# The output's columns taken with a stride of four, stores of whole 512-byte runs, and a written order for three engines in the last layers of an fp32 attention and two-MLP kernel

## The chip, the core and the metric

One NeuronCore of a Trainium2 chip runs the whole program. The metric is device time of one execution in microseconds (us). A change of less than about 0.3% (3.5 us here) can't be told from none.

## What is computed

```python
def _attn_ref(q, k, v, mem_k, mem_v):          # (4, 8, 768, 64), 8 memory slots
    for c in range(768 // 32):                 # chunks of 32 queries, window 16 + 32 + 8
        ...
        a = softmax(scale * q_c @ concat(mem_k, k_ctx).T)
        out[:, :, c_start:c_end] = a @ concat(mem_v, v_ctx)

x = attn_out.transpose(0, 2, 1, 3).reshape(3072, 512)
h = x @ w_in                                   # 512 x 2048
x = np.maximum(0.01 * h, h) @ w_out            # 2048 x 512
y = ((x @ w_a) * (x @ w_b)) @ moe2_w_out       # 512 x 1536, twice, then 1536 x 512
```

All arrays are fp32; y has 3072 rows (tokens) of 512 columns, so a row is 2 KB.

## The kernel before

**Numbers.** An fp32 operand is kept as two parts, `hi` (a rounded copy) and `lo` (the rest), and a product is three matmuls: lo·hi, hi·lo, hi·hi. ScalarE (ACT) makes `hi` with a cast, VectorE (DVE) makes `lo` with a subtraction.

**Stages.** Attention and the first MLP run over six blocks of 512 tokens (`TB`). Beside them `prep_steps` (L676) reads w_a, w_b and the second w_out, forms the sums of their quarters that a seven-product scheme (Strassen's, in Winograd's form) needs, splits them and stores them in DRAM (`wabd`, `wtd`). The scheme replaces the eight products of a 2 by 2 block product by seven, numbered `i` = 0 to 6.

**The last layers.** They run over three super-blocks `sb` of 1024 tokens (two halves `h` of 512), and in each over six pairs `p` of 128-column tiles of w_a and w_b. For a pair, `layer3(k, m)` (L885) makes the seven products with w_a (`m` = 0), then the seven with w_b (`m` = 1), six matmuls of 512 columns each. They go to the PSUM banks `ca`, `cb`, `cc`; a bank goes on being summed into after ACT has copied its state into a tile `u` (`snap`, L892): `u2` after product 4, `u3` after product 5. So PE may start product 5 only after the `u2` copy, and product 2 only after the `u3` copy. DVE combines banks and copies into `ga` (w_a side) and, multiplied by it, `gb`. The four `gb` quarters then give seven operands `st`: ACT casts (`cast`, L900), DVE subtracts (`low`, L906), with four DVE additions between them (c22, c21, c11, c12).

Two pairs form a group `g`. Its output product is 14 units (`unit`, L1033): 7 products for each of two 128-column tiles `dt` of w_out, six matmuls each into `oa`, `oy` or `oz`, after which DVE (or ACT, for the first group) adds the bank to `acc`. Units of a group run between the products of the next pair; a super-block's last group runs among the first products of the next super-block, or alone at the end of the program.

**The change of super-block.** The operands of the next super-block (`xc_make`, L755: `ch` by ACT, `cl` by DVE, `t1` to `t4` by DVE, each of 1024 columns) are made while the last group runs. Finished `acc` tiles are transposed by DVE in 32 by 32 blocks (`turn`, L1043) into `y` and stored: for each of the eight (h, e, dt) tiles of a super-block four stores of 32 columns by 512 tokens, 64 KB each, in runs of 32 columns, 128 bytes. This happens during the next super-block's pairs 0 and 1, or at the end of the program.

**What sets the order.** PE follows the order of the text in all of this part (`InOrder`, L31, `pe.on`). DVE and ACT follow it only around the ends of super-blocks (`dve.on`, `act.on`); elsewhere the framework's scheduler orders them by priority. SyncE (SP) issues all loads and stores, in the order that the scheduler gave: weights `wab` (512 KB, two products each, a ring of 5 tiles, `wab_load` L838), output weights `wt` (`wt_load` L859), the `xs` loads and the stores. A DMA whose buffer or data is not ready holds up every later one on SP. Which products and units alternate is written in the table `PLAN` (L1066) and the main loop (L1075).

Of the kernel before, what the change touches and what calls it, by code (L numbers as in the profile page):

```python
# [14 lines left out]
P = 128  # L15
# [38 lines left out]
def kernel(  # L54
# [621 lines left out]
    def prep_steps():  # L676
        n = 0
        for p in range(NF2 // 2):
            for m in range(3):
# [6 lines left out]
                z11, z12 = z[:, 0, 0:256], z[:, 0, 256:512]  # L686
                z21, z22 = z[:, 1, 0:256], z[:, 1, 256:512]
# [8 lines left out]

                def comb(c, x, y, op):
                    nc.vector.tensor_tensor(out=t[:, c], in0=x, in1=y, op=op)
# [8 lines left out]
                else:  # L707
                    plain(0, 1, z11)
                    plain(1, 2, z[:, 1, :])
# [38 lines left out]
    def xc_parts(sb, i, t):  # L748
        hi = xq.tile([P, HC, TB], F32R, tag=f"ch{i}", name=f"ch{i}")
        lo = xq.tile([P, HC, TB], F32R, tag=f"cl{i}", name=f"cl{i}")  # L750
        two = "p k n -> p (k n)"
        w_parts(hi.rearrange(two), lo.rearrange(two), t.rearrange(two), dve)
        xc[sb, i] = (hi, lo)

    def xc_make(sb, i):  # L755
# [7 lines left out]
        if i == "t1":  # L763
            sub(b12, b12, b11)
        elif i == "t2":
            sub(b12, b22, b12)
        elif i == "t3":
            sub(b11, b12, b11)
        elif i == "t4":
            sub(b21, b21, b12)  # L770
        else:
            xc_parts(sb, i, (b11, b21, b21, b12, b12, b11, b22)[i])
# [110 lines left out]
    ga, gb, later = {}, {}, {}  # L883

    def layer3(k, m):  # L885
# [4 lines left out]
        ends = p == NP - 1  # L890
# [19 lines left out]
        def done(k, h, ps, t=None):  # L910
# [24 lines left out]
            c11, c12, c21, c22 = gb[0, 0], gb[1, 0], gb[0, 1], gb[1, 1]  # L935
            if not ends or sb + 1 < NS:
                low(1, c12)
            tt(c22, c21, c22, ALU.add)
            cast(3, c22)
            tt(c21, c11, c21, ALU.subtract)  # L940
            low(3, c22)
            tt(c11, c22, c11, ALU.subtract)
            cast(4, c11)
            tt(c12, c12, c11, ALU.subtract)
            low(4, c11)
            cast(6, c12)
            cast(5, c21)
# [24 lines left out]
        u2 = snap(A, "u2")  # L972
        yield
# [7 lines left out]
        if m and ends:  # L981
            later[2] = lambda: low(2, gb[1, 1])
# [3 lines left out]
        if m and ends:  # L986
            later[1] = lambda: low(1, gb[1, 0])
        yield
        product(C, n + 6, sb, 6, False)
        done(0, 1, C, u2)  # L990
        yield
        if m:
            low(6, gb[1, 0])
            low(5, gb[0, 1])
# [4 lines left out]
    def mul(sb, g, dt, i, seed=False):  # L999
        if i == 0:  # L1000
# [11 lines left out]
        for k in range(2):  # L1012
            c, w = st[sb, 2 * g + k, i], wts[sb, g, i][:, k]
            kw = dict(skip_group_check=True)
            pe.matmul(ps, w[:, 1, q], c[:, 0], start=begins and k == 0, stop=False, **kw)
            pe.matmul(ps, w[:, 0, q], c[:, 1], start=False, stop=False, **kw)
            pe.matmul(ps, w[:, 0, q], c[:, 0], start=False, stop=k == 1, **kw)
# [3 lines left out]
    def add(sb, g, dt, i):  # L1021
# [4 lines left out]
        acc = accs[sb, h][:, e, dt]  # L1026
        ps = {3: oy, 6: oy, 1: oz}.get(i, oa)[dt]
# [33 lines left out]
    def stage(k, m, pos):  # L1061
        if made.get((k, m), 0) == pos:
# [3 lines left out]
    PLAN = (  # L1066
        {3: ((0, 0),), 4: ((0, 3), (0, 1)), 5: ((0, 4),)},
        {
            0: ((0, 6),), 6: ((0, 5),), 7: ((1, 0), (0, 2)), 2: ((1, 3), (1, 4)),
            3: ((1, 1), (1, 5)), 4: ((1, 6), (1, 2)),  # L1070
        },
    )

    pe.on, pe.last = True, None
    for k, (sb, p) in enumerate(pairs):  # L1075
# [3 lines left out]
        for m in range(2):  # L1079
            end = p == NP - 1 and m == 1  # L1080

            def units(pos):
                if not odd and p:
                    for u in PLAN[m].get(pos, ()):
                        unit(sb, g - 1, *u)

            for pos in range(6):
                held = p == 4 and sb + 1 < NS and m == 0 and pos == 5
                if held:
                    dve.on, dve.last = True, None  # L1090
                stage(k, m, pos)
                if held:
                    xc_make(sb + 1, "t1")
                    dve.on = False
                units(pos)
                if pos == 1 and (k or m):
                    for e in (6, 7, 8):
# [168 lines left out]
```

## Time and profile before

| | |
|---|---|
| median of 3 runs | 1169.02 us (1168.79 to 1171.77) |
| the profiled execution, its own time | 1166.6 us |
| its span, first to last instruction | 1164.8 us |
| PE busy | 1117.6 us, 96% |
| DVE, ACT busy | 722.1 us (62%), 498.2 us (43%) |
| last layers | from about 606 us to the end |
| stores of the output | 53.4 thousand packets of less than 512 bytes in the last layers, queue issues 96 x 64 KB |

The profile is one execution. Its page gives busy shares by engine, slices in time and a chain of waits followed back from the last instruction; the trace behind it gives windows, timelines of single instructions and DMA queues. Matmul ends are modelled (0.39 us shown for one that the next follows after 0.227 us), so idle times of PE in the rows are short of the time lost by 0.16 us; the start of one row and of the next is the safer measure.

### The profile page before, as it was taken

The page shows a single profiled execution, that of the slowest core. Times are in us where ns is not written, and L with a number is a line of the kernel's source. Part 1 is how long each engine was busy: PE and PEld are TensorE (multiplying, and loading weights), DVE is VectorE, ACT ScalarE, POOL GpSimd, SP SyncE. Part 2 cuts the span into 40 slices and gives each one's busy share as a digit, 9 for nine tenths or more (in the row PEclk, how much of TensorE's full clock was granted, in tenths as well). Part 3 has the DMA queues.
Part 4 walks back from the last instruction along what each step waited for, and adds up shares of the span by engine and source line. Part 5 has one row for each costly group of instructions (what it writes and reads, how often), then busy time and mean ns, then how long its engine had stood idle before and what let it go on. Part 6 is the DMA issues. An engine that isn't in the chain of part 4 may idle for free.

```text
span 1164.8 us, 16365 instructions
## 1 busy us (share of the span) xinstructions
PE 1117.6 (96%) x6236; PEld 918.6 (79%) x6236; DVE 722.1 (62%) x1325; ACT 498.2 (43%) x831; POOL 6.3 (1%) x16
## 2 busy tenths in 40 slices
PE   7899999999999999999999999999799999799994
PEld 6788888888878888888888888877688887588873
DVE  6896588779768946544105556678446578436574
ACT  5886555455455543343223432324333233334140
POOL 2000000000000000000000000000000000000000
PEclk9999999999999999999999999999899999899997
DMA  9996899999999984244339474767774766856534
GB/s 315 392 357 227 289 327 331 336 314 335 326 319 335 321 293 136 92 178 166 115 138 329 144 247 139 243 189 173 234 235 145 236 181 172 213 178 208 177 99 72
DMA packets 136462, 269.58 MB, mean 231 GB/s; under 512 B 59840, under 2 KB 60992, under 8 KB 135616
## 3 DMA queue, kind: packets, MB, share of 16 engines
q1 hardware_dynamic: 136304, 268.41, 70.3%
q8 instruction: 49, 0.80, 0.3%
q14 instruction: 29, 0.24, 0.1%
q10 hardware_dynamic: 80, 0.13, 0.0%
HBM read 214.50 MB, written 54.00 MB: 231 GB/s over the span
## 4 chain that ended last, share of the span: by engine, by line
PE 87%; DVE 4%; DMA 3%; ACT 3%; SPq 1%; issue 0%; DVEq 0%; ACTq 0%
PE ca L47 14%; PE oa L47 8%; PE h L410 8%; PE a L530 7%; PE a L534 7%; PE a L533 7%; PE h L411 7%; PE h L412 7%; PE cc L47 7%; PE oy L47 4%; PE cb L47 4%; DVE gb L898 3%; PE pv L383 2%; PE s L274 2%; DMA wab<-wab 2%; PE oz L47 1%
## 5 line engine op out<-in xcount | busy, mean ns | idle before, releaser
L47 PE MATMUL ca<-ch,wab 128*128 128x512 f32 x575 | 198.8, 398 | 18.1 <-DMA wab<-wab 14.7
L410 PE MATMUL h<-xh,w 128*128 128x512 f32 (+1 forms) x384 | 151.5, 395 | 0.7 <-ACT xh L47 0.7
L530 PE MATMUL a<-gh,w 128*128 128x512 f32 (+1 forms) x392 | 150.7, 384 | 0.8 <-ACT x L547 0.8
L533 PE MATMUL a<-gl,w 128*128 128x512 f32 (+1 forms) x392 | 150.4, 384 | 0.0
L534 PE MATMUL a<-gh,w 128*128 128x512 f32 (+1 forms) x392 | 150.4, 384 | 0.0
L411 PE MATMUL h<-xl,w 128*128 128x512 f32 (+1 forms) x384 | 148.5, 387 | 0.2 <-DVE xl L47 0.2
L412 PE MATMUL h<-xh,w 128*128 128x512 f32 (+1 forms) x384 | 148.5, 387 | 0.0
L47 PEld LDWEIGHTS ca<-ch,wab 128*128 128x128 f32 x575 | 109.6, 191 | 48.7 <-DMA wab<-wab 16.6
L508 DVE TENSOR_TENSOR gl<-g,gh 128x512 fp32r<-128x512 f32 (+1 forms) x96 | 65.4, 681 | 104.6 <-ACT gh L505 100.5
L47 PE MATMUL ca<-cl,wab 128*128 128x512 f32 x288 | 113.7, 395 | 1.5 <-DVE cl L47 1.5
L903 ACT CAST st<-gb 128x512 fp32r<-128x512 f32 x111 | 67.5, 621 | 107.3 <-DVE gb L898 104.9
L502 ACT ACTIVATE g<-h 128x512 f32<-128x512 f32 (+1 forms) x96 | 56.3, 587 | 128.2 <-PE h L412 127.2
L47 PE MATMUL oa<-st,wt 128*128 128x512 f32 x432 | 106.9, 389 | 0.0
L47 PE MATMUL cc<-ch,wab 128*128 128x512 f32 x288 | 100.4, 389 | 0.0
L47 PEld LDWEIGHTS oa<-st,wt 128*128 128x128 f32 x432 | 80.9, 188 | 17.2 <-DVE acc L47 0.4
L530 PEld LDWEIGHTS a<-gh,w 128*128 128x128 f32 x392 | 73.6, 188 | 16.1 <-ACT x L547 1.5
L534 PEld LDWEIGHTS a<-gh,w 128*128 128x128 f32 x392 | 73.7, 188 | 14.5
L533 PEld LDWEIGHTS a<-gl,w 128*128 128x128 f32 x392 | 73.6, 188 | 14.5
L410 PEld LDWEIGHTS h<-xh,w 128*128 128x128 f32 x384 | 72.1, 188 | 16.3 <-ACT xh L47 0.8
L898 DVE TENSOR_TENSOR st<-gb,st 128x512 fp32r<-128x512 f32 x108 | 73.2, 689 | 17.3 <-ACT st L903 16.5
L412 PEld LDWEIGHTS h<-xh,w 128*128 128x128 f32 x384 | 72.1, 188 | 14.7
L411 PEld LDWEIGHTS h<-xl,w 128*128 128x128 f32 x384 | 72.2, 188 | 14.2 <-DVE xl L47 0.5
(155 smaller groups left out, 1627.6 us busy)
## 6 DMA issues: line engine op xcount, KB each, us to landing
wab<-wab SPq DMA_DIRECT2D x126, 512.0 KB, 4.4
w<-wod SPq DMA_DIRECT2D x80, 512.0 KB, 4.6
raw<-w SPq DMA_DIRECT2D x68, 512.0 KB, 7.0
wt<-wtd SPq DMA_DIRECT2D x63, 512.0 KB, 4.4
k<-kl SPq DMA_DIRECT2D x48, 256.0 KB, 5.2
v<-vl SPq DMA_DIRECT2D x48, 256.0 KB, 5.1
wab<-pwb SPq DMA_DIRECT2D x12, 768.0 KB, 6.9
wod<-w SPq DMA_DIRECT2D x16, 512.0 KB, 6.4
```

Source lines behind the costliest of these rows:

```text
L47: self.last = emit(*args, **kwargs).ins
L274: pe.matmul(s[64 * cpar:64 * cpar + 64, cp * 4 + hp, :], qb[:, o, :], k[:, r:r + 64], start=True, stop=True,)
L410: pe.matmul(ps, w[1], x[0], start=first, stop=False)
L411: pe.matmul(ps, w[0], x[1], start=False, stop=False)
L412: pe.matmul(ps, w[0], x[0], start=False, stop=last)
L502: act.activation(g[:, c], ps[:, c], AF.Prelu, alpha=0.01)
L508: dve.tensor_tensor(out=gl[:, c], in0=g[:, c], in1=gh[:, c].bitcast(F32), op=ALU.subtract)
L530: pe.matmul(ps, slot[:, 1, c], gh[:, t], start=f == 0 and o == 0, stop=False, **kw)
L533: pe.matmul(ps, slot[:, 0, c], gl[:, t], start=False, stop=False, **kw)
L534: pe.matmul(ps, slot[:, 0, c], gh[:, t], start=False, stop=f == NF1 - 1 or (o == HALF and f == LEAD - 1), **kw)
L898: dve.tensor_tensor(out=out, in0=x, in1=y, op=op)
L903: act.copy(w[:, 0, :], t)
```

## The change

1. The weights of the last product are prepared with other columns (`prep_steps`, w_out only): instead of the quarters [0:256] and [256:512], quarter `e` and tile `dt` take the columns 4n + 2dt + e. The casts and subtractions read them with a step of four fp32 (16 bytes); one piece of two quarters becomes two pieces.
2. `turn` writes `y` with that same step, so that 128 neighbouring columns of a token stand together. A new `store` writes 128 columns by 512 tokens, 256 KB in 512-byte runs: 8 stores a super-block instead of 32, each once all four (e, dt) of a half are turned.
3. PE, DVE and ACT follow the text's order through all of the last layers. `PLAN` is written out; the tail of `layer3` is cut into more steps (the additions with product 6; then casts 3 and 4; then casts 6 and 5), and these are put at other places.
4. `xc_make` can make `hi` and `lo` apart. At a change of super-block one output unit (tile 1, product 2) moves to between products 4 and 5, and the operands are made in another order.
5. At the end of the program each half's stores follow its turns; the last unit is cut into two of 256 tokens, whose stores go half on SP and half on ACT's queue.

```diff
-                z11, z12 = z[:, 0, 0:256], z[:, 0, 256:512]
-                z21, z22 = z[:, 1, 0:256], z[:, 1, 256:512]
+                if m < 2:
...
+                else:
+                    (z11, z12), (z21, z22) = [
+                        [z[:, k].rearrange("p (n d e) -> p e d n", d=2, e=2)[:, e] for e in range(2)]
+                        for k in range(2)
+                    ]
...
-                    plain(0, 1, z11)
-                    plain(1, 2, z[:, 1, :])
+                    plain4(0, z11)
+                    plain4(1, z21)
+                    plain4(2, z22)
...
             if (k, h) != (0, 1):
-                i = {(0, 0): 0, (1, 0): 1, (1, 1): 2}[k, h]
-                cast(i, o)
-                if i == 0 or i == 2 and not ends:
-                    low(i, o)
-                return
...
+                cast({(0, 0): 0, (1, 0): 1, (1, 1): 2}[k, h], o)
...
         product(C, n + 6, sb, 6, False)
+        if m:
+            low(1, gb[1, 0])
         done(0, 1, C, u2)
+        if m:
+            c11, c12, c21, c22 = gb[0, 0], gb[1, 0], gb[0, 1], gb[1, 1]
+            tt(c22, c21, c22, ALU.add)
+            tt(c21, c11, c21, ALU.subtract)
         yield
         if m:
-            low(6, gb[1, 0])
-            low(5, gb[0, 1])
+            cast(3, c22)
+            low(3, c22)
+            tt(c11, c22, c11, ALU.subtract)
+            cast(4, c11)
+            tt(c12, c12, c11, ALU.subtract)
+            low(4, c11)
         yield
+        if m:
+            cast(6, c12)
+            cast(5, c21)
+            low(6, c12)
+            low(5, c21)
+        yield
...
-    def turn(sb, h, e, dt, src=None):
+    def turn(sb, h, e, dt, src=None, b=slice(0, 16)):
         if (sb, h) not in ys:
-            ys[sb, h] = xp.tile([P, 2, 2, TB], F32, tag="xh", name="y")
-        y = ys[sb, h][:, e, dt]
-        dve.transpose(out=y, in_=accs[sb, h][:, e, dt] if src is None else src)
+            ys[sb, h] = xp.tile([P, 16, 32, 4], F32, tag="xh", name="y")
+        if src is None:
+            src = accs[sb, h][:, e, dt]
+        dve.transpose(out=ys[sb, h][:, b, :, 2 * dt + e], in_=src[:, 32 * b.start:32 * b.stop])
+
+    def store(sb, h, a, eng, b=slice(0, 16)):
         t0 = (2 * sb + h) * TB
-        for a in range(4):
-            f0 = 256 * e + P * dt + 32 * a
-            nc.sync.dma_start(
-                out=out[t0:t0 + TB, f0:f0 + 32].rearrange("(b i) j -> i b j", i=32),
-                in_=y[32 * a:32 * a + 32].rearrange("i (b j) -> i b j", j=32),
-            )
+        rows = out[t0 + 32 * b.start:t0 + 32 * b.stop, P * a:P * a + P]
+        eng.dma_start(
+            out=rows.rearrange("(b i) f -> i b f", i=32),
+            in_=ys[sb, h][32 * a:32 * a + 32, b].rearrange("i b j c -> i b (j c)"),
+        )
...
-    pe.on, pe.last = True, None
+    for e in (pe, dve, act):
+        e.on, e.last = True, None
...
+            i = {(0, 1): n - 2, (1, 0): n + 2, (1, 1): n + 6}.get((p, m), -1)
+            if sb and n >= 2 and 0 <= i:
+                if i < 8:
+                    turn(sb - 1, *TURNS[i])
+                if i >= 4:
+                    store(sb - 1, i // 4 - 1, i % 4, nc.sync)
...
+        m = 0
+        stage(k, m, 0)
+        stage(k, m, 1)
+        before(6, 7)
+        stage(k, m, 2)
+        stage(k, m, 3)
+        before(8)
...
+        stage(k, m, 4)
...
+        stage(k, m, 5)
+        before(9)
...
+            for hb in range(2):
+                t, b = slice(256 * hb, 256 * hb + 256), slice(8 * hb, 8 * hb + 8)
+                M(1, 2, False, t)
+                E(1, 2, t)
+                turn(sb, 1, 0, 1, None, b)
+                for a in range(4):
+                    store(sb, 1, a, (nc.sync, nc.scalar)[a % 2], b)
```

`before(n)` runs step n of the previous seven products' `layer3`; `M` and `E` are a unit's matmuls and its addition.

**SP, around the stores of the first super-block.** The number after `wab` is that of the pair's weights in DRAM: 111 is pair 0, 112 pair 1, 113 pair 2 of the second super-block. Before:

```order
L842 DMA wab<-wab_112 128x1024 x3
L1051 DMA out<-y 32x16x32 x12
L842 DMA wab<-wab_112 128x1024
L1051 DMA out<-y 32x16x32 x4
L842 DMA wab<-wab_112 128x1024 x2
L1051 DMA out<-y 32x16x32 x8
L842 DMA wab<-wab_112 128x1024
L1051 DMA out<-y 32x16x32 x8
L842 DMA wab<-wab_113 128x1024 x4
```

Now:

```order
L869 DMA wab<-wab_112 128x1024 x4
L1081 DMA out<-y 32x16x128
L869 DMA wab<-wab_112 128x1024 x2
L1081 DMA out<-y 32x16x128
L869 DMA wab<-wab_112 128x1024
L1081 DMA out<-y 32x16x128 x2
L869 DMA wab<-wab_113 128x1024 x2
L1081 DMA out<-y 32x16x128
```

The first tile of pair 2 stood behind all 32 stores of the super-block; it stands behind four of the eight now.

**ACT, in the first products of an odd pair** (pair 3 of the first super-block; the first `u` row is its `u2` copy, the second its `u3` copy, and the casts belong to the pair before). Before:

```order
L903 CAST st<-gb 128x512 x2
L914 COPY ga<-cb 128x512
L903 CAST st<-gb 128x512
L894 COPY u_6707<-ca 128x512
L903 CAST st<-gb 128x512 x3
L894 COPY u_6728<-ca 128x512
```

Now:

```order
L47 CAST st<-gb 128x512
L47 COPY ga<-cb 128x512
L47 COPY u_6705<-ca 128x512
L47 CAST st<-gb 128x512 x2
L47 COPY u_6734<-ca 128x512
L47 CAST st<-gb 128x512 x2
```

Two of the casts that stood ahead of the `u3` copy stand behind it, and the cast that stood ahead of the `u2` copy stands behind that.

**PE, at the change from the first super-block to the second.** `oa` rows are output units of the old super-block; `ca` rows with `ch_7402` (before) and `ch_7397` (now) are the end of the new one's product 4, and the next `ch` its product 5. Before:

```order
L47 MATMUL ca<-ch_7402,wab 128x512 x2
L47 MATMUL ca<-cl_7403,wab 128x512
L47 MATMUL ca<-ch_7402,wab 128x512
L47 MATMUL ca<-ch_7424,wab 128x512
L47 MATMUL ca<-cl_7425,wab 128x512
```

Now:

```order
L47 MATMUL ca<-ch_7397,wab 128x512 x2
L47 MATMUL ca<-cl_7399,wab 128x512
L47 MATMUL ca<-ch_7397,wab 128x512
L47 MATMUL oa<-st,wt 128x512 x6
L47 MATMUL ca<-ch_7415,wab 128x512
L47 MATMUL ca<-cl_7418,wab 128x512
```

A unit of six matmuls, which ran with the other `oa` units before product 1, stands between products 4 and 5.

## Rows read from the trace of the kernel before

**Rows 1.** Windows: length, busy us (instructions) of each engine, granted PE clock, DMA share, GB/s.
```profile
260.00:280.00 20.00, 20.00 (x144) 16.55 (x144) 18.91 (x44) 13.16 (x20) 0.00 (x0) 1.00 0.94 331
...
820.00:840.00 20.00, 15.89 (x62) 12.98 (x63) 8.99 (x14) 5.87 (x11) 0.00 (x0) 0.83 0.82 295
...
779.75:832.85 53.10, 43.93 (x180) 34.63 (x180) 32.94 (x49) 18.48 (x30) 0.00 (x0) 0.94 0.82 223
965.10:1018.20 53.10, 44.08 (x183) 34.81 (x182) 33.47 (x50) 18.85 (x31) 0.00 (x0) 0.94 0.75 189
```

**Rows 2.** Chain of waits in order of time: start us, us, what.
```profile
824.11 4.91 PE ca L47 x12
829.01 1.36 PE cc L47 x6
```

**Rows 3.** Timeline of SP, second super-block's pairs 0 and 1: start us, us, issues.
```profile
795.05 7.75 SPq L1051 DMA_DIRECT2D out<-y  x12
...
815.21 4.78 SPq L1051 DMA_DIRECT2D out<-y  x8
```

**Rows 4.** Timeline of PE: start us, us, instruction [idle before <-releaser].
```profile
632.38 0.50 PE L47 MATMUL ca<-ch,wab 128*128 128x512 f32 x1 [0.20 <-ACT u L894]
...
686.96 0.47 PE L47 MATMUL ca<-ch,wab 128*128 128x512 f32 x1
...
690.14 0.50 PE L47 MATMUL ca<-ch,wab 128*128 128x512 f32 x1 [0.20 <-ACT u L894]
...
784.54 0.50 PE L47 MATMUL ca<-ch,wab 128*128 128x512 f32 x1 [0.73 <-ACT u L47]
...
789.08 0.50 PE L47 MATMUL ca<-cl,wab 128*128 128x512 f32 x1 [0.76 <-DVE cl L47]
...
824.11 0.79 PE L47 MATMUL ca<-ch,wab 128*128 128x512 f32 x1 [7.12 <-DMA wab<-wab]
...
1118.06 0.50 PE L47 MATMUL ca<-ch,wab 128*128 128x512 f32 x1 [0.21 <-ACT u L894]
```

**Rows 5.** Timeline of ACT in the odd pair whose product 5 starts at 686.96.
```profile
686.29 0.58 ACT L894 COPY u<-ca 128x512 f32<-128x512 f32 x1
687.74 1.87 ACT L903 CAST st<-gb 128x512 fp32r<-128x512 f32 x3 [0.87 <-DVE gb L898]
689.52 0.58 ACT L894 COPY u<-ca 128x512 f32<-128x512 f32 x1
```

**Rows 6.** Timeline of PE, SP and DVE at the end of the program.
```profile
1142.97 5.60 PE L47 MATMUL oa<-st,wt 128*128 128x512 f32 x24
...
1144.52 17.77 SPq L1051 DMA_DIRECT2D out<-y  x32
...
1149.22 2.48 DVE L47 STREAM_TRANSPOSE y<-acc 128x512 f32<-128x512 f32 x4
```

**Rows 7.** DMA, 1144 to 1165 us: packets, MB, share of 16 engines; issue to landing.
```profile
q1 hardware_dynamic: 16896, 2.10, 58.4%
...
out<-y SPq DMA_DIRECT2D x32, 64.0 KB, 1.9
```

**Rows 8.** DMA, 860 to 900 us, weights alone, in the same columns.
```profile
q1 hardware_dynamic: 2160, 7.84, 62.3%
...
wab<-wab SPq DMA_DIRECT2D x11, 512.0 KB, 4.2
```

**Rows 9.** Groups by shape: count | busy us, mean ns of one | idle before.
```profile
L898 DVE TENSOR_TENSOR gb<-gb 128x512 f32<-128x512 f32 x60 | 41.4, 690 | 1.4
...
L246 ACT COPY qz<-qr 64x512 f32<-64x512 f32 x20 | 21.8, 1090 | 10.4 <-PE s L274 10.3
...
L117 DVE SCALAR_TENSOR_TENSOR pz<-raw,pz 128x512 int32<-128x512 int32 x36 | 24.9, 692 | 1.1
...
L1047 DVE STREAM_TRANSPOSE y<-acc 128x512 f32<-128x512 f32 x16 | 10.3, 685 | 0.0
```

**Rows 10.** PE's waits from 100 to 600 us: total, times, longest.
```profile
PE a L530 <- ACT x L547: 0.8, 1, 0.8
```

More of the change, by code (lines that the diff above doesn't have):

```diff
@@ new lines, with now, x, before @@
+        rows = not odd and p
+        def now(m, *us):
+            if rows:
+                units(sb, g - 1, *us)
+        def x(i, part=None):
+            if sb + 1 < NS:
+                xc_make(sb + 1, i, part)
+        def before(*ns):
+            if k or m:
+                for n in ns:
+                    stage(*((k, 0) if m else (k - 1, 1)), n)
+        def beside(m, n):
+            if odd and not m:
+                for r in (n, 6)[:1 + (n == 5)]:
+                    wt_load(sb, g, r)
+            i = {(0, 1): n - 2, (1, 0): n + 2, (1, 1): n + 6}.get((p, m), -1)
[4 more added lines that the diff above has]
+                    store(sb - 1, i // 4 - 1, i % 4, nc.sync)
@@ new lines @@
+        m = 0
+        stage(k, m, 0)
+        beside(m, 0)
+        stage(k, m, 1)
+        beside(m, 1)
+        before(6, 7)
+        stage(k, m, 2)
+        beside(m, 2)
+        stage(k, m, 3)
+        before(8)
+        now(m, (0, 0))
+        beside(m, 3)
+        stage(k, m, 4)
+        now(m, (0, 3), (0, 1))
+        beside(m, 4)
+        if rows:
+            before(9)
+        if p == NP - 1:
+            x("t1")
+        stage(k, m, 5)
+        before(9)
+        now(m, (0, 4))
+        beside(m, 5)
@@ new lines @@
+        m = 1
+        stage(k, m, 0)
+        stage(k, m, 1)
+        now(m, (0, 6))
+        if p == NP - 1:
+            x(0)
+        before(6)
+        now(m, (0, 5))
+        before(7, 8, 9)
+        now(m, (1, 0), (0, 2))
+        stage(k, m, 2)
+        now(m, (1, 3), (1, 4))
+        beside(m, 2)
+        stage(k, m, 3)
+        now(m, (1, 1), (1, 5))
+        if p == NP - 1:
+            x(1)
+        beside(m, 3)
+        stage(k, m, 4)
+        now(m, (1, 6), (1, 2))
+        beside(m, 4)
@@ L1159, with M, E @@
+        stage(k, m, 5)
+        beside(m, 5)
+        if p < NP - 1:
+            continue
+        def M(dt, i, *args):
+            mul(sb, g, dt, i, *args)
+        def E(dt, i, *args):
+            add(sb, g, dt, i, *args)
+        units(sb, g, (0, 0))
+        if sb + 1 == NS:
+            seed(sb, 0)
             stage(k, m, 6)
-            later[2]()
-            M(1, 0)
+            units(sb, g, (1, 0))
+            seed(sb, 1)
             stage(k, m, 7)
-            E(1, 0)
-            stage(k + 1, 0, 0)
@@ new lines @@
+            break
+        stage(k, m, 6)
+        units(sb, g, (1, 0))
+        stage(k, m, 7)
+        stage(k + 1, 0, 0)
+        stage(k, m, 8)
+        M(0, 1)
+        M(1, 1)
+        units(sb, g, (0, 3))
+        stage(k, m, 9)
+        x(3, 0)
+        units(sb, g, (1, 3), (0, 4))
+        E(0, 1)
+        units(sb, g, (1, 4))
+        E(1, 1)
+        stage(k + 1, 0, 1)
+        x(6, 0)
+        x(3, 1)
+        x("t2")
+        M(0, 6)
+        M(1, 6)
+        units(sb, g, (0, 5))
+        x(4)
@@ L1203, in _layout @@
+        x("t3")
+        units(sb, g, (1, 5))
+        M(0, 2)
+        x(5, 0)
+        E(0, 6)
+        x(5, 1)
+        stage(k + 1, 0, 2)
+        x("t4")
+        E(1, 6)
+        stage(k + 1, 0, 3)
+        stage(k + 1, 0, 4)
+        x(2, 0)
+        M(1, 2)
+        x(2, 1)
+        stage(k + 1, 0, 5)
+        x(6, 1)
+        E(0, 2)
+        E(1, 2)
 def _layout(np, q, k, v, mem_k, mem_v):
```

216 lines of the change are left out of this document (66 added, 150 removed).

## The prediction

> **What bounds the kernel now.** PE is busy for 96% of the span, so I read first where it waits. From 100 to 600 us it waits 0.8 us in all [rows 10]: the early layers have nothing to give. In the last layers six matmuls take 1.36 us [rows 2], 0.227 us each, and a window with its count of matmuls shows what is lost. Three places lose.
>
> *The changes of super-block.* The two windows of 53.10 us hold 180 and 183 matmuls [rows 1]; at 0.227 us that is 40.8 and 41.5 us of work, so 12.3 and 11.6 us are lost. The timeline of PE shows the kinds in the first one: waits for the `u2` copy and for the operand `cl` (0.73 and 0.76 us idle), then 7.12 us for a tile of weights [rows 4]. After that last wait twelve matmuls take 4.91 us in place of 2.72 [rows 2], and the granted clock of that stretch is 0.83 [rows 1]: the engine idled, fell to the lower of its two levels, 1.2 GHz, and came back. The tile was late because of SP: twenty of the 32 stores fill 7.75 and 4.78 us of its time [rows 3], and the tile is asked for behind the last of them, at 820 us.
>
> *Odd pairs.* From 632.38 to 1118.06 us there are seven waits of some 0.2 us idle for the `u3` copy [rows 4]. From start to start the one at 690.14 costs more: product 5 starts at 686.96, so twelve matmuls later, at 689.68, product 2 was due; it came 0.46 us late, and its first, slower matmul adds 0.1. I take 0.55 each, 3.9 us in all. ACT shows why: the copy runs at 689.52, behind three casts that had waited for DVE [rows 5].
>
> *The end.* PE ends at 1148.6, DVE at 1151.7. SP issues the 32 stores one every 0.555 us until 1162.3 [rows 6], and the last lands some 2 us later [rows 7]. So 16 us of the span come after the last matmul, bound by issues.
>
> **The change, part by part.** *The tile behind the stores.* Eight stores replace 32, with as many runs each, so I take the same 0.555 us of SP each: 4.4 us, not 17.8. The first tile of pair 2 stands behind four of them. By the order, its buffer is free after pair 1's product 2, five products (6.8 us) before it is needed, and a load lands in 4.2 us [rows 8]: 2.6 us to spare. The DMA engines could still crowd it. A 128-byte packet takes 58.4% of 16 engines times 21 us over 16,896, 11.6 ns [rows 7]; a 4 KB one, some 1,910 of them in 62.3% of 16 times 40 us, 208 ns [rows 8]. The price of 512 bytes isn't in the trace: it lies between 11.6 ns and four times that, 46; the straight line between the two rows gives 30.6, which I take, since both ends are measured. Pair 1 lasts 14 products, 19.0 us, and asks for seven loads of 128 packets (1.66 us each, 11.6) and 4,096 packets of stores (7.8): 19.4 us, which the 2.6 to spare cover. So this wait goes, and the fall of the clock with it.
>
> *The operands at the change.* The unit moved between products 4 and 5 gives the `u2` copy 1.36 us of cover where 0.73 was missing. I stepped the new DVE and ACT rows through with 0.69 us for DVE's 512 columns, 0.58 for a copy [rows 9, 5] and twice that for 1024: `cl` of product 2 is made some 1 us before its use, product 6's about 0.2. DVE takes the transposes one or two at a time between the `gb` steps, all in the 8 us that it has free there (53.1 - 32.9 busy, less the 12.3 that vanish [rows 1]). Late next would be the `u3` copy in pair 1. Of the 23.9 us lost at both changes I count 23.1 as won.
>
> *Odd pairs.* SP and PE keep their order; ACT's changes. The `u2` copy can start as soon as product 4 is out, about 685.8, and cast 3 follows at 686.4. DVE subtracts its `lo` (until 687.7) and only then makes c11 (688.4); cast 4 ends at 689.05 and the `u3` copy at 689.65, against 689.68 where PE needs it. The other two casts come behind it. So 0.55 shrinks to nothing or 0.1: 3.2 of 3.9 us. The three engines' order elsewhere costs nothing by the same stepping: between units PE has over 2 us more.
>
> *The end.* DVE has the same eight transposes and seven additions; stepped with the rows it ends with the last half tile at 1150.7. The second half's stores are then issued in four steps on two queues, by 1151.9 at 0.555 each (ACT's issue as SP's, and all descriptors priced as before), and land 1.9 later: 1153.8. The data are the other limit: 4,096 packets at 30.6 ns take 7.8 us from the first store's data at about 1147: 1155, which I take. 9.8 us won, between 6.5 (late transposes, below) and 11.2.
>
> *Costs.* Twelve matmuls of 256 columns replace six of 512: at best no more time, at worst 1.4 us if each took as long; 0.1 taken, as half the columns should take near half. `hi` and `lo` made apart are the same work. The preparation of w_out's columns has, six times, one more cast and one more subtraction, under 0.7 us each [rows 9], and reads with a step of 16 bytes. The nearest rows are a DVE read at 8 bytes, 692 ns against 690 without a step, and an ACT read at 64 bytes, 1090 against 580 [rows 9, 5]; so between 0.3 and 3 us of DVE or ACT each. PE covers it, having waited 0.8 us in 500 [rows 10]; in the fullest stretch DVE is busy 18.9 of 20 us [rows 1], so up to 2 us could show, and 0.2 is taken. SP's loads of the early layers don't move.
>
> **Sum.** 23.1 + 3.2 + 9.8 - 0.1 - 0.2 = 35.8 us: the profiled execution would go from 1166.6 to 1130.8. The median of the runs shown is 2.4 above that execution, so I forecast 1169.0 - 35.8 = **1133 us**.
>
> **The rivals.** *Scattered transposes.* `turn` writes single elements 16 bytes apart. No row shows DVE doing that. For it speak the 1090 against 580 ns of ACT at 64 bytes, against it DVE at 8 bytes without a price. At ACT's ratio a transpose takes 1.27 us, 0.58 more. In pair 1 two stand ahead of cast 4, so the `u3` copy comes about 1.1 us late, at each change; at the end eight take 4.7 us more, of which the data's limit hides 2: 1133 + 2.2 + 2.7 = 1138. The Trainium skill speaks for this one (Advanced Engine Details and Errata, section SBUF Cachelines): it gives lines of 16 bytes, wants two hits on each, and warns of a penalty for another line at every access, which is this step exactly. By that rule the trace's two strided rows agree, as 8 bytes hit each line twice and 64 once; whether it holds for what DVE writes, no row shows.
>
> *Stores still crowd the weights.* At 46 ns a packet pair 1 needs 11.6 + 11.9 = 23.5 us of the DMA engines for 19.0: the tile comes 2 to 4.5 us late at each change, and the end's data take 4 more: 1133 + 8 + 4 = 1145. For it speaks the DMA share of 0.82 in the window [rows 1], against it that much of that share was small packets.
>
> *The odd pairs keep their wait*, the order not doing what it is written for: the `u3` copy has 0.03 us to spare in my stepping, and one handover more would be 0.5. 1133 + 3.2 = 1136.
>
> *Slower.* Scattered transposes so dear that they take the place of what is removed. With e more for each, a change costs eight e less the 8 us that DVE has free, the end eight e less 2: 24 e - 18. It decides from 24 e - 18 = 35.8 + 3.5, e = 2.4, a transpose of 3.1 us, 4.5 times the row; at five times the kernel takes 1133 + 48 = 1181. For it speaks only that the pattern is new, against it ACT's ratio of 1.9.
>
> **How the numbers follow.** Forecast 0.46, odd pairs' wait kept 0.16, scattered transposes 0.21, crowded DMA 0.10, slower 0.03; 0.04 for what I don't see. The best the rows allow is 23.9 + 3.9 + 11.2 = 39 us, 1130; with 1.5 us for the measurement the range starts at 1128. It ends at 1144, which holds the first three cases and most of the fourth, and leaves 1 in 10 to 2 in 10. Faster than the bound 0.94, same 0.03, slower 0.03.
>
> **What would show it.** Right: windows of the two changes with some 234 matmuls in 53 us and a granted clock of 1.00; no idle of PE on `wab`; the `u3` copy of odd pairs no later than 2.7 us after product 5 starts; transposes near 685 ns; the span's end some 6 us after the last matmul. Wrong: transposes above 1 us, PE waiting for `u` or `st` where it didn't before, loads of `wab` landing in over 6 us beside the stores, or more than 2 us of PE's waits before 600 us.

## The result, and the profile after

| | before | changed |
|---|---|---|
| median (runs) | 1169.66 us (1168.79 to 1171.77, 4) | 1135.67 us (1134.03 to 1136.39, 4) |
| ratio, 95% interval | | 0.9705 (0.9687 to 0.9723) |
| profiled execution: time, span | 1166.6, 1164.8 us | 1135.98, 1134.2 us |
| PE busy | 96% | 98% |
| end of the last matmul | 1148.6 us | 1128.57 us |

34 us of medians are gone, 1.8 us fewer than forecast; between the profiled executions it is 30.6, because the one of before lies 3 us under its median. Of these 30.6, 20.0 stand before the end of the last matmul and 10.6 behind it (16.2 us of span followed it, 5.6 do now). But PE's last matmul is itself late now, by 3.9 us (below), so the second figure is too high as the end's gain. Counted from the start of the program's last four units, 1142.97 [rows 6] and 1118.97, to the end of the span, the end is 6.6 us shorter (21.8 and 15.2).

PE's waits from 600 us to the end in the kernel before (total, times, longest; two for `ch`, 0.5 us in all, left out):

```profile
PE ca L47 <- DMA wab<-wab: 14.7, 4, 7.1
PE ca L47 <- DVE cl L47: 1.5, 2, 0.8
PE ca L47 <- ACT u L47: 1.5, 2, 0.7
PE ca L47 <- ACT u L894: 1.4, 7, 0.2
```

and in the changed kernel from 600 to 1130 us:

```profile
PE oa L47 <- DVE acc L47: 2.7, 1, 2.7
PE cc L47 <- DVE ga L47: 2.5, 4, 1.0
PE ca L47 <- ACT u L47: 0.4, 2, 0.2
```

No wait for weights (`wab`) and no wait for `cl` is left, and `u` is waited for twice instead of nine times. New are four waits for `ga` and one, at the end, for `acc`.

The two changes of super-block, in windows of the same 53.10 us as [rows 1] (length, busy us and instructions of PE, PEld, DVE, ACT, POOL, granted clock, DMA share, GB/s):

```profile
780.30:833.40 53.10, 51.88 (x227) 42.30 (x227) 39.38 (x55) 21.43 (x37) 0.00 (x0) 1.00 0.78 246
954.03:1007.13 53.10, 51.88 (x227) 42.30 (x227) 39.38 (x55) 21.43 (x37) 0.00 (x0) 1.00 0.71 206
```

227 matmuls stand where 180 and 183 did, at a clock of 1.00 instead of 0.94. At 0.227 us each that is 51.5 us of work, so 1.6 us are still lost in each, of 12.3 and 11.6: 20.7 us won.

SP in the first change (start, us, issues), to be held against [rows 3]:

```profile
796.79 0.34 SPq L1081 DMA_DIRECT2D out<-y  x1
...
799.51 0.42 SPq L1081 DMA_DIRECT2D out<-y  x1
...
802.23 0.95 SPq L1081 DMA_DIRECT2D out<-y  x2
806.43 3.02 SPq L869 DMA_DIRECT2D wab<-wab  x2
```

The first tile of pair 2 is asked for at 806.43, where it was 820; its product starts at 814.38. A load lands in 5.1 us here (median from 790 to 825 us), so 2.8 us are to spare; 2.6 were forecast. A store takes SP 0.34 to 0.48 us, not 0.555.

All three engines where PE waits for `ga`:

```profile
804.11 0.58 ACT L47 COPY u<-ca 128x512 f32<-128x512 f32 x1
804.85 2.00 DVE L47 STREAM_TRANSPOSE y<-acc 128x512 f32<-128x512 f32 x2
806.70 0.67 DVE L47 TENSOR_TENSOR ga<-u,cc 128x512 f32<-128x512 f32 x1
807.42 0.50 PE L47 MATMUL cc<-ch,wab 128*128 128x512 f32 x1 [1.03 <-DVE ga L47]
```

`ga` needs `u`, ready at 804.69, but DVE is at two transposes until 806.7, and PE's product 6 waits for `ga`. By the starts of PE's matmuls this costs 1.3 us at each change, and a short wait for the `u3` copy just before it 0.5 more. Before, the PE stall for weights lay behind this place. The other two waits for `ga` (0.23 us idle, 0.5 with the slower first matmul, at 748.50 and its like a super-block later) have the operand difference `t1` of 1.22 us in front of the same addition.

ACT in the odd pair of [rows 5]:

```profile
685.77 0.59 ACT L47 COPY u<-ca 128x512 f32<-128x512 f32 x1 [0.83 <-PE ca L47]
686.26 0.62 ACT L47 CAST st<-gb 128x512 fp32r<-128x512 f32 x1
688.24 0.62 ACT L47 CAST st<-gb 128x512 fp32r<-128x512 f32 x1 [1.36 <-DVE gb L47]
688.77 0.58 ACT L47 COPY u<-ca 128x512 f32<-128x512 f32 x1
689.25 1.14 ACT L47 CAST st<-gb 128x512 fp32r<-128x512 f32 x2
```

The `u3` copy ends at 689.35; product 5 started at 686.88, so product 2 is due twelve matmuls later, at 689.60, and starts then. All seven such waits are gone.

Groups of DVE and ACT by shape (count | busy us, mean ns | idle before), against [rows 9]:

```profile
L47 DVE STREAM_TRANSPOSE y<-acc 128x512 f32<-128x512 f32 x21 | 21.8, 1075 | 0.0
L716 DVE TENSOR_TENSOR ps<-pz 128x256 f32<-128x256 f32 x36 | 16.9, 485 | 0.3
L123 ACT CAST pwa<-pz 128x256 fp32r<-128x256 f32 x30 | 15.6, 551 | 14.1 <-DMA wab<-pwa 10.7 <-DVE pz L117 2.7 <-DVE gl L508 0.7
```

A transpose that writes with a step of 16 bytes takes 1075 ns where it took 685.

The end of the program, against [rows 6]:

```profile
1118.97 5.30 PE L47 MATMUL oa<-st,wt 128*128 128x512 f32 x24
...
1122.74 8.71 SPq L1081 DMA_DIRECT2D out<-y  x8
...
1124.65 1.96 DVE L47 STREAM_TRANSPOSE y<-acc 128x512 f32<-128x512 f32 x2
1126.47 0.40 DVE L47 TENSOR_TENSOR acc<-acc,oa 128x256 f32<-128x256 f32 x1
...
1126.92 1.65 PE L47 MATMUL oa<-st,wt 128*128 128x256 f32 x6 [2.66 <-DVE acc L47]
```

PE's second half of the last unit goes to the bank that DVE reads for the first half's addition. That addition is queued behind two transposes, and PE waits 2.66 us. From 1118.97 to PE's end it is 9.6 us; run e7, where PE waits for none of this, takes 5.67 for the same matmuls. So PE's end is 3.9 us late. The DMA queues from 1118 to 1135 us (packets, MB, share of 16 engines), against [rows 7]:

```profile
q1 hardware_dynamic: 3200, 1.57, 34.7%
q10 hardware_dynamic: 1088, 0.52, 12.1%
```

46.8% of 16 engines times 17 us over 4,288 packets are 29.7 ns for a packet; 30.6 was taken.

### The profile page after: what moved, and what is told of

Same layout as the page of the kernel before. It is cut to its first block, busy times and chain, and to the rows that moved or that the text cites. A ratio compares the mean times of both kernels' runs of the same rounds, so it can differ in the third digit from the quotient of the medians.

```text
span 1134.2 us, 16303 instructions
## 1 busy us (share of the span) xinstructions
PE 1111.6 (98%) x6242; PEld 919.4 (81%) x6242; DVE 739.1 (65%) x1333; ACT 499.2 (44%) x837; POOL 6.3 (1%) x16
## 4 chain that ended last, share of the span: by engine, by line
PE 91%; DVE 5%; ACT 2%; DMA 1%; issue 0%; SPq 0%; DVEq 0%; ACTq 0%
PE ca L47 15%; PE oa L47 8%; PE cc L47 8%; PE h L410 8%; PE a L530 8%; PE a L534 8%; PE a L533 8%; PE h L411 7%; PE h L412 7%; PE cb L47 4%; PE oy L47 4%; PE pv L383 2%; PE s L274 2%; DVE gb L47 2%; PE oz L47 1%; DVE y L47 1%
## 5 line engine op out<-in xcount | busy, mean ns | idle before, releaser
L47 PE MATMUL ca<-ch,wab 128*128 128x512 f32 x575 | 192.2, 389 | 0.4 <-ACT u L47 0.4
L47 ACT CAST st<-gb 128x512 fp32r<-128x512 f32 x126 | 76.5, 621 | 130.4 <-DVE gb L47 129.8
L47 PE MATMUL oa<-st,wt 128*128 128x512 f32 (+1 forms) x438 | 108.4, 389 | 2.7 <-DVE acc L47 2.7
L47 DVE TENSOR_TENSOR st<-gb,st 128x512 fp32r<-128x512 f32 x126 | 85.2, 688 | 15.8 <-ACT st L47 14.5
L410 PEld LDWEIGHTS h<-xh,w 128*128 128x128 f32 x384 | 72.1, 188 | 16.2 <-ACT xh L47 0.8
L412 PEld LDWEIGHTS h<-xh,w 128*128 128x128 f32 x384 | 72.1, 188 | 14.7
```

The lines of the kernel that those rows point to most:

```text
L47: self.last = emit(*args, **kwargs).ins
L410: pe.matmul(ps, w[1], x[0], start=first, stop=False)
L412: pe.matmul(ps, w[0], x[0], start=False, stop=last)
```

## The experiments

| run | median (us) | ratio to before, 95% interval |
|---|---|---|
| changed kernel | 1135.67 | 0.9705 (0.9687 to 0.9723) |
| e1_runs32 | 1132.56 | 0.9679 (0.9666 to 0.9692) |
| e2_stores_only | 1150.13 | 0.9827 (0.9814 to 0.9841) |
| e3_order_only | 1158.87 | 0.9905 (0.9890 to 0.9920) |
| e4_casts_first | 1146.68 | 0.9796 (0.9782 to 0.9811) |
| e5_unit_back | 1139.72 | 0.9742 (0.9729 to 0.9756) |
| e6_h0_two_queues | 1132.09 | 0.9677 (0.9663 to 0.9691) |
| e7_pe_no_wait | 1132.67 | 0.9689 (0.9674 to 0.9703) |
| e8_all_mended | 1129.37 | 0.9654 (0.9640 to 0.9667) |
| e9_unit_whole | 1131.80 | 0.9677 (0.9663 to 0.9691) |
| e10_h0_sooner | 1130.11 | 0.9659 (0.9646 to 0.9672) |

The theory at the start: the stores' issues had held up the weights and the end, the order had held up the operands and odd pairs, and the new transposes take a part back. The rivals: the order does it all; the longer transposes come from work beside them.

**e1_runs32: the same stores, without scattered writes.** The four 32-column blocks of a run of 128 come from the four (e, dt) tiles; the columns' order in w_out follows.

```diff
-                        [z[:, k].rearrange("p (n d e) -> p e d n", d=2, e=2)[:, e] for e in range(2)]
+                        [z[:, k].rearrange("p (a d e j) -> p e d a j", d=2, e=2, j=32)[:, e] for e in range(2)]
...
-            ys[sb, h] = xp.tile([P, 16, 32, 4], F32, tag="xh", name="y")
+            ys[sb, h] = xp.tile([P, 16, 4, 32], F32, tag="xh", name="y")
...
-        dve.transpose(out=ys[sb, h][:, b, :, 2 * dt + e], in_=src[:, 32 * b.start:32 * b.stop])
+        dve.transpose(out=ys[sb, h][:, b, 2 * dt + e], in_=src[:, 32 * b.start:32 * b.stop])
```

> The changed kernel with output columns in blocks of 32: transposes write runs of 32 elements (128 bytes) in place of single elements 16 bytes apart, stores still write 512-byte runs, and the preparation reads runs of 32. Order as changed. Theory (the scattered write is what makes a transpose 1075 ns): 128x512 transposes back at 685 ns (within 20); the two PE waits on ga behind two transposes (1.3 us each) fall below 0.6; at the end DVE is some 3 us earlier; the whole takes 1131 to 1132.5 us against 1135.7. Rival (the transposes are longer because of what runs beside them, or the second difference, the preparation, carries it): transposes stay above 950 ns, time within 1 us of 1135.7.

Groups of DVE and ACT in this run, and one of PE's waits from 600 us on:

```profile
L716 DVE TENSOR_TENSOR ps<-pz 128x256 f32<-128x256 f32 x36 | 14.6, 418 | 0.3
L47 DVE STREAM_TRANSPOSE y<-acc 128x512 f32<-128x512 f32 x21 | 14.2, 695 | 0.0
L123 ACT CAST pwa<-pz 128x256 fp32r<-128x256 f32 x30 | 11.1, 402 | 15.5 <-DMA wab<-pwa 12.1 <-DVE pz L117 3.4
...
PE ca L47 <- DMA wab<-wab: 1.2, 1, 1.2
```

Transposes are back at 695 ns and the time is 3.1 us lower; no run of the one kernel reaches into those of the other (1132.18 to 1133.11), though 3.1 us are less than 0.3% and the two intervals overlap at their ends. The two larger waits for `ga` shrink from 1.03 to 0.35 us idle, and the wait at the end from 2.66 to 1.59. The theory holds: the scattered write is what makes a transpose long. 0.39 us for each of 24 transposes is 9.4 us of DVE, of which a third shows.

Two more things differ between the traces and blur the size. The last layers began 1.4 us sooner here (603.78, against 605.23), and PE waits once, near 640 us, for weights. That wait stands in e3 and e6 too and in no other run; its cause is open. Run e7 has the same transposes and no such wait. From the start of its last layers (605.36) to its end it takes 525.7 us, the changed kernel 528.9: by that count the scattered writes cost 3.2 us, some 2.2 at the two changes and 1.1 at the end.

**e2_stores_only: the kernel before with the new columns, `turn` and `store`.** All else, the order of DVE and ACT too, is as before.

```diff
-                if sb and 2 <= pos and (p, m) in ((0, 1), (1, 0)):
-                    turn(sb - 1, *TURNS[4 * p + pos - 2])
+                i = {(0, 1): pos - 2, (1, 0): pos + 2, (1, 1): pos + 6}.get((p, m), -1)
+                if sb and pos >= 2 and 0 <= i:
+                    if i < 8:
+                        turn(sb - 1, *TURNS[i])
+                    if i >= 4:
+                        store(sb - 1, i // 4 - 1, i % 4, nc.sync)
...
                 turn(sb, 0, 1, 1)
+                for a in range(4):
+                    store(sb, 0, a, nc.sync)
                 turn(sb, 1, 1, 1)
+                for a in range(4):
+                    store(sb, 1, a, nc.sync)
```

> The kernel before with the new columns, transposes and 512-byte stores (8 a super-block, at the changed kernel's places; at the end of the program all on SP), and the old order of DVE and ACT. Theory (the stores carry the two waits for a tile of weights, 9.5 us each with the slower clock behind them, and most of the end, some 6; the order carries the operands' and odd pairs' waits): no wait of PE on wab in the two changes, granted clock 1.00 there, the seven 0.5 us waits on u still there, 1143 to 1147 us. Rival (the order is needed too: without it the weights come late all the same): waits on wab of over 2 us remain and the time is 1152 us or more.

PE's waits from 600 us on, and then the end:

```profile
PE ca L47 <- ACT u L913: 2.8, 9, 0.7
PE ca L47 <- DVE cl L47: 1.5, 2, 0.8
PE ca L47 <- ACT u L47: 1.5, 2, 0.7
PE cc L47 <- DVE gb L917: 1.3, 2, 0.7
```

```profile
1134.42 3.75 DVE L47 STREAM_TRANSPOSE y<-acc 128x512 f32<-128x512 f32 x4
1137.30 7.17 SPq L1072 DMA_DIRECT2D out<-y  x8
```

No wait on `wab` is left without the new order: the stores alone carry that. The old waits for `u` and `cl` stay, as expected. New are a wait for `gb` and one for `u` in pair 1 of each change; DVE is at four transposes (3.78 us from 796.17 on) ahead of that `gb`. The time was missed by 3 to 7 us, for the most part at the end: the last matmul ends at 1133.2, yet 15.3 us follow it. The last transposes come in a row, the first half is complete only at 1137.3, and no store can go sooner. With 512-byte runs a store needs all four tiles of its half, so the order of the transposes decides when data start.

**e3_order_only: the changed kernel with the old columns and stores.**

```diff
-        dve.transpose(out=ys[sb, h][:, b, :, 2 * dt + e], in_=src[:, 32 * b.start:32 * b.stop])
+        y = ys[sb, h][:, e, dt, c]
+        dve.transpose(out=y, in_=src[:, c])
+        for a in range(4):
+            f0 = 256 * e + P * dt + 32 * a
+            nc.sync.dma_start(
...
```

> The changed kernel with the old columns and the old stores (64 KB, 128-byte runs, 32 a super-block): the order alone. Theory: the waits on wab come back at both changes (7 us each and a slower clock behind them) and the end is again bound by 32 issues, 16 us after the last matmul; only odd pairs (3.9) and part of the operands' waits (up to 3.6) are won: 1160 to 1165 us. Rival (the order carries most of the gain): 1150 us or less.

```profile
PE ca L47 <- DMA wab<-wab: 18.6, 5, 8.6
PE oa L47 <- DVE acc L47: 1.6, 1, 1.6
PE cc L47 <- DVE ga L47: 0.4, 2, 0.2
```

In PE's waits from 600 us on (above) those for weights are back, longer than before (14.7 us in all there): PE reaches the missing tile sooner, and 1.0 us is the wait near 640 us that e1 has too. Those for `u` and `cl` are gone: they hang on the order alone. By medians 11 us are won, a little more than expected; 12.6 us stand behind the last matmul in place of 16.2, but here too PE's last matmul is late, and from the start of the last four units on the end is 1.7 us shorter. The parts alone give 20.2 us (1 - 0.9827, of 1170) and 11.1; together they give 34.5 (1 - 0.9705), so by medians 3 us need both. The traces, from the start of the last layers to the end, put the parts at 16.3 and 6.2 and the whole at 31.2. Of the 8.7 us that need both by that count, 4.0 lie at the end (0.9 won in e2, 1.7 here, 6.6 with both): whole runs are worth little there until the order completes a half early, as e2's last rows show. The rest lies before it, where e3 waits longer for weights and e2 has its new waits in pair 1.

**e4_casts_first: casts 6 and 5 ahead of the `u3` copy again.** One `yield` moves, so that these casts come with 3 and 4.

```diff
             low(4, c11)
-        yield
-        if m:
             cast(6, c12)
...
             low(5, c21)
         yield
+        yield
```

> The changed kernel with casts 6 and 5 and their lows put back ahead of the next product's u3 copy (in the step of casts 3 and 4). Theory (these two casts ahead of the copy are what made PE wait in odd pairs): each of the seven odd pairs waits 0.5 us for u again, and the pairs after a change as well, 3.5 to 5 us in all: 1139 to 1141 us. Rival (those waits went for another reason, the earlier u2 copy or the order of DVE): no waits on u beyond the changed kernel's, within 1 us of 1135.7.

```profile
PE ca L47 <- ACT u L47: 9.0, 9, 1.4
PE cc L47 <- DVE ga L47: 3.0, 4, 1.1
```

The waits for `u` are back, at nine places, but at 0.9 to 1.4 us each, those for `ga` grow by 0.5 in all, and the time is 11 us up instead of 3.5 to 5. The odd pair's ACT and PE rows show why it is dearer than before the change:

```profile
687.52 0.59 ACT L47 COPY u<-ca 128x512 f32<-128x512 f32 x1 [0.83 <-PE ca L47]
...
689.98 1.87 ACT L47 CAST st<-gb 128x512 fp32r<-128x512 f32 x3 [1.36 <-DVE gb L47]
...
691.76 0.58 ACT L47 COPY u<-ca 128x512 f32<-128x512 f32 x1
...
692.39 0.50 PE L47 MATMUL ca<-ch,wab 128*128 128x512 f32 x1 [0.88 <-ACT u L47]
```

From copy to copy it is 4.24 us here, 3.23 before the change [rows 5], 3.00 with it: the additions now follow product 6 and cast 3 follows the `u2` copy, so the three casts start later than in the old order. The part that the prediction named decides, and it is worth more inside the new order than the old waits were.

**e5_unit_back: the unit (1, 2) in front of the new product 1 again.**

```diff
         M(0, 2)
+        M(1, 2)
         x(5, 0)
...
         x(2, 0)
-        M(1, 2)
         x(2, 1)
```

> The changed kernel with the unit (tile 1, product 2) put back in front of the new super-block's product 1 at each change, as before; all else as changed. Theory (the moved unit covers the u2 copy): PE waits 0.9 us more for u at each change and nothing moves behind it, 1137 to 1138 us against 1135.7. Rival (the place of the unit does nothing, another wait hides it): PE's time lost in the changes is that of the changed kernel, within 0.7 us of 1135.7.

```profile
775.53 1.66 PE L47 MATMUL oa<-st,wt 128*128 128x512 f32 x6 [1.05 <-DVE acc L47]
...
782.00 0.50 PE L47 MATMUL ca<-ch,wab 128*128 128x512 f32 x1 [0.73 <-ACT u L47]
```

PE's rows at the first change show the 0.73 us for `u2` back to the digit [rows 4]. The other row was not expected: in its old place the unit also waits for DVE to read its bank, since the additions stand later in the new order. 4 us in all, twice what I gave the move.

**e6_h0_two_queues: at the end, the first half's stores on two queues** (on top of e1).

```diff
-                store(sb, 0, a, nc.sync)
+                store(sb, 0, a, (nc.sync, nc.scalar)[a % 2])
```

> The kernel of run e1_runs32 with the first half's four stores at the end of the program issued in turn on SP and ACT in place of SP alone. Theory (from the first store on the end is bound by the data of 2.1 MB, and one queue moved it at some 205 GB/s where two moved some 280): the first half's data are out 1.3 us sooner, 1130.8 to 1131.6 us against 1132.6. Rival (the end is bound by the last half's turns and their stores, not by what goes before): within 0.5 us of 1132.6.

The GB/s that the core's DMA engines moved, in 40 slices: e1 from 1115 to 1132 us,

```profile
GB/s 0 0 0 0 0 0 0 0 0 0 0 0 0 90 207 205 204 204 184 175 300 280 262 245 286 290 193 280 255 293 300 277 99 152 157 0 0 0 0 0
```

and e6 from 1115 to 1131:

```profile
GB/s 0 0 0 0 0 0 0 0 0 0 0 0 0 42 211 205 205 205 200 169 260 288 268 250 275 277 293 313 314 178 204 323 314 316 135 3 0 0 0 0
```

The theory fell: the first 2.5 us run at 205 GB/s with two queues as with one, and the 0.5 us of difference between the medians can't be told from none. The traces agree on half a us, though: from the first store's issue to the end it is 11.2 us in e1 and e7, 10.7 in e6 and e8, the two with two queues. Why the flow begins at that rate stays open.

**e7_pe_no_wait: both halves of the last unit's matmuls ahead of the first half's addition** (on top of e1).

```diff
+            for t, b in halves:
+                M(1, 2, False, t)
             turn(sb, 1, 1, 1)
             turn(sb, 1, 0, 0)
-            for hb in range(2):
-                t, b = slice(256 * hb, 256 * hb + 256), slice(8 * hb, 8 * hb + 8)
-                M(1, 2, False, t)
+            for t, b in halves:
                 E(1, 2, t)
```

> The kernel of run e1_runs32 with both halves of the last unit's matmuls written ahead of the first half's addition, so that PE does not wait for it. Theory (the end is bound by data and by DVE's turns, and PE's wait costs nothing): PE's last matmul ends some 1.5 us sooner and the time stays within 0.7 us of 1132.6. Rival (the wait is on the path): the 1.6 us go, 1130.7 to 1131.3 us.

```profile
1116.98 5.67 PE L47 MATMUL oa<-st,wt 128*128 128x512 f32 x30
```

PE's wait is gone, its last matmul ends at 1122.65 instead of 1124.49, and the median is the same (1132.67). From the first store's issue to the end it is 11.2 us in both traces: PE's longest wait in the last layers of e1 cost nothing.

**e8_all_mended: e6 and e7 together, and two things that DVE did ahead of `ga`, one transpose and `t1`, put behind it.** The diff shows the second part alone.

```diff
-        if p == NP - 1:
-            x("t1")
         stage(k, m, 5)
         before(9)
+        if p == NP - 1:
+            x("t1")
...
-                if i < 8:
-                    turn(sb - 1, *TURNS[i])
+                for j in {6: (), 7: (6, 7)}.get(i, (i,) if i < 8 else ()):
+                    turn(sb - 1, *TURNS[j])
```

> The kernel of run e1_runs32 with four things at once: the two queues of e6, the order of e7, one transpose of pair 1 put behind the u3 copy's addition instead of ahead of it, and the operand difference t1 of pair 5 put behind that addition. Theory: PE's four waits for ga (0.5 us each with the slower matmul behind) go, 2 us, and the end wins 1.3: 1128.5 to 1130 us, the fastest. Rival (what is moved is late elsewhere): new waits of over 1 us in the changes, 1131.5 us or more.

Its windows of the two changes:

```profile
779.80:832.90 53.10, 53.10 (x236) 43.77 (x235) 37.12 (x56) 22.02 (x38) 0.00 (x0) 1.00 0.78 247
951.20:1004.30 53.10, 53.10 (x235) 43.76 (x234) 37.16 (x56) 22.03 (x38) 0.00 (x0) 1.00 0.70 207
```

PE is busy for all of both windows; from 605 us on the view of its waits is empty. This is the fastest version, 6.3 us under the changed kernel, with intervals that don't meet. What is left of the last layers is PE's work, and 8 us behind it.

**e9_unit_whole and e10_h0_sooner: what sets the end** (both on top of e8). The first leaves the last unit whole:

```diff
-            for t, b in halves:
-                M(1, 2, False, t)
...
+            units(sb, g, (1, 2))
+            turn(sb, 1, 0, 1)
...
```

The second completes the first half sooner:

```diff
-            units(sb, g, (0, 5))
+            M(0, 5)
             turn(sb, 0, 1, 1)
...
+            E(0, 5)
```

> The kernel of run e8_all_mended with the last unit whole (six matmuls of 512 columns, one addition, one transpose, four stores of 256 KB in turn on SP and ACT) instead of two halves of 256 tokens. Theory (the end is bound by the data of the stores once they flow, and by the moment at which the last half's first data may leave): the second half's first store goes 0.4 to 0.5 us later, and the data behind it are the same, so 0.4 to 1 us longer, 1129.8 to 1130.4 us against 1129.4. Rival (the cut was worth what the prediction put on the end's issues, several us): 1131.5 us or more.

> The kernel of run e8_all_mended with the last transpose of the first half at the end put ahead of the addition of the unit (tile 0, product 5), so that the first half's stores may go some 0.65 us sooner. Theory (the 2.1 MB flow without a gap from the first store to the end, so the first store's time sets the end): 0.4 to 0.7 us sooner, 1128.7 to 1129.0 us, and the stores' first issue 0.6 us sooner in the trace; PE does not wait for the addition. Rival (the last half's turns on DVE set the end): no change, the data show a gap between the halves.

The whole unit costs 2.4 us by medians and 1.2 in the traces, counted from the start of the last layers: more than my 0.4 to 1, well short of the rival. So the cut looks like a gain; the two intervals still touch, and its size isn't settled. In e10 the first store goes 0.66 us sooner, counted from the same start, and the time stays (the intervals lie on each other). The data from 1116 to 1131 us show the gap of which the rival spoke:

```profile
GB/s 0 0 0 0 0 0 0 0 0 57 214 203 203 206 199 184 210 294 279 255 257 187 64 201 203 150 195 273 309 314 316 208 331 253 27 0 0 0 0 0
```

The 64 in the middle is the gap: the first half is out before the second half's data are ready. So in e8 a sooner first half wins nothing: the end then waits for the second half's data. Whether a sooner second half would win was not tried.

## Why the prediction was right, point by point

*The tile behind the stores: right.* The 7 us waits and the slower clock behind them are gone, with 2.8 us to spare where 2.6 were worked out, and e2 and e3 show that the stores do it and the order doesn't. The price of a packet, taken on the line between two rows, was 29.7 ns in place of 30.6, and the rival of the crowded DMA fell with it.

*The operands at the change: right in kind.* The `u2` and `cl` waits went, and e5 brings the first one back. The sum had 23.1 us for both changes; 20.7 came, and the windows hold 227 matmuls where some 234 were named.

*Where the step failed* is "DVE takes the transposes one or two at a time between the `gb` steps, all in the 8 us that it has free there". The total was free, but not the moment: two transposes ahead of `ga` are late for PE's product 6. At 695 ns this costs little (0.35 us idle in e1, 0.6 by the starts), at 1075 it is 1.03 (1.3, and 0.5 for `u`). This is the rival of scattered transposes, which came true, and with it two of the prediction's signs of being wrong: transposes above 1 us, and PE waiting for `u` where it didn't before. The rival had named the `u3` copy as the place in pair 1; the longer wait is at `ga`. By ACT's ratio a transpose was to take 0.58 us more and the kernel 2.2 + 2.7; it takes 0.39 more, and at that size the rival's own sum is 1.5 (2.2 x 0.39 / 0.58) and 1.1 (eight times 0.39, less 2): 2.6 us. Measured are 3.1 by e1's median and 3.2 by the traces (2.2 and 1.1). That the changed kernel lies 2.7 over the forecast, near the rival's sum, is in part chance: other terms missed too, in both directions (below). I held it for less likely than the forecast, by the DVE row at 8 bytes without a price; the ACT row at 64 bytes was the nearer guide. The Trainium skill (Advanced Engine Details and Errata, section SBUF Cachelines) warns of a penalty for another 16-byte line at every access; the trace agrees, for a DVE write as well, 1075 against 695 ns with runs of 32 elements.

*Odd pairs: right.* 3.2 was forecast, 3.9 came: none of the seven waits is left, and the `u3` copy has 0.25 us to spare, not 0.03. e4 shows that the two casts behind the copy decide.

*"The three engines' order elsewhere costs nothing" was wrong by 1.0 us:* `t1` ahead of `ga` in pair 5, 0.5 at each change. I had stepped the rows through from the last pair's end on, and `t1` comes before that.

*The end: right in kind, too high by 3.2 us.* Its issues no longer bind, but of 9.8 us only 6.6 came, the low edge of the range that was given for it (6.5). The 10.6 us behind the last matmul hold PE's own delay of 3.9, which I did not see: PE waits for the first half's addition. By e7 that wait costs nothing, but it moves the mark from which the end is counted: without it the sign of "some 6 us after the last matmul" would have shown 9.5. With transposes that write runs the end wins 7.7 (e1, e7), so scattered writes took 1.1. The other 2.1 lie in the data: in e1 they flow from 1120.7 to 1129.9, 9.1 us where 7.8 were taken, and the span ends 1.2 us after them, which the sum left out. The price of a packet was right, as time of a busy engine; not all 16 were busy all the time, and e10's gap shows that the second half's transposes limit the flow too. The bounds also don't follow from their own terms: an end at 1153.8 wins 11.0, not 11.2, and 9.8 less 2.7 is 7.1, not 6.5.

*The small costs.* The 256-column cut was put at 0.1 us of loss for PE, and PE's last matmuls take 5.67 us (e7) for 5.60 [rows 6]; for the whole end e9 points to a gain. The preparation's strided reads were mis-sized: between the groups of the changed kernel and of e1 they take 8.1 us more of DVE (2.3 and 2.3 for L716, 3.5 for L124) and 4.5 of ACT (L123), where 3 was the upper bound for each. Means are 485 against 418 ns and 551 against 402, and in both groups only a part reads with the step: 18 casts and 42 operations of DVE in all, at some 0.65 us against 0.40 and 0.62 against 0.42. The ACT row's ratio of 1.9 did bound a strided cast (1.6); it would have given some 6 us for 18 of them, so the bound of 3 was too low for the count. The DVE row at 8 bytes had no price and was no guide. PE still covers it, as far as can be seen: the last layers began between 602.3 and 607.3 us in all these executions, in no order that goes with the reads.

*The sum, and luck.* Between the profiled executions 35.8 us were forecast and 30.6 came. From the start of the last layers (604.66, now 605.23) to the last four units 24.6 us are won: 20.7 for the changes and 3.9 for odd pairs, less 1.0 for `t1`, are 23.6, and 1.0 I can't place. With 6.6 at the end, less 0.6 by which the early layers ended later, that is the 30.6. So the forecast was 5.2 us too high, 2.4 at the changes and 3.2 at the end above all. That the median came within 2.7 us of it is in part luck: the two medians differ by 3.4 us more than the profiled executions do, because the profiled one of the kernel before is faster than any of its other runs here, and no trace of a slower one shows where those 3.4 us lie.

## What to carry to other kernels

A queue that issues loads and stores in one order can make a store's issue time a wait for weights, as here: fewer, longer stores then gain far from where they stand. Free time of an engine over a stretch doesn't say that a new instruction is free: look which short addition stands right behind it, and who waits for that. When an engine's last instruction has moved, count the end from a mark that has not. When a layout is changed for the DMA's sake, check that the engine that fills it still writes runs; here blocks of 32 give the same 512-byte stores without the price.

## What was not expected of the hardware

- A DVE transpose of 128x512 fp32 that writes single elements 16 bytes apart takes 1075 ns, 1.55 times the 695 of one that writes runs of 32 elements; of 128x256, 631 against 445.
- The end's stores flow at 200 to 214 GB/s for their first 2 to 2.5 us and mostly at 245 to 325 later (e1, e6), with one issuing queue as with two. No run here shows why.
- A 256 KB store took 0.34 to 0.48 us of SP between the loads of weights, against 0.56 to 0.65 for one of 64 KB before ([rows 3, 6]). At the end SP took 1.09 on the mean of eight, four of them of 128 KB, but there its time holds waits for the transposes too.
